# Attention and gated MLP on one core: V evicted into its own partition half, two copies per chunk, and all engines in a new order

## The chip, the core and the metric

One NeuronCore of one Trainium2 chip. The metric is device time in microseconds of one execution, the median over several runs. Engines: TensorE (PE), which multiplies matrices; ScalarE (ACT); VectorE (DVE); GpSimd (POOL); SyncE (SP), which here only issues DMAs. A *chunk* is 512 of the 2048 positions, a *tile* 128 of them.

## What is computed

```python
xn = _layernorm(x, axis=-1)                  # x: [1, 2048, 512], bf16
q = (xn @ wq).reshape(B, S, 32, 16)          # 32 heads of 16
k, v = xn @ wk, xn @ wv                      # one K and V head for all
p = softmax(q @ k^T * 16 ** -0.5)            # per head, 2048 x 2048
s = (p @ v) @ wo
g = silu(silu(xn @ w1) @ w2)                 # MLP, F = 1792
return x + s * g
```

## The kernel before

**Tiling.** Scores are made transposed, keys on partitions and 512 queries in the free dimension, for groups of two heads and 64 keys at a time: one *score group* is four matmuls of 64 rows by 32 columns (lines 1025 to 1036; where the keys stand in the array already, the weight load is left out, line 1030). There are 32 head groups `g` and 64 such score tiles in each, 2048 in all.

**Two ways to the exponential.** A score tile in a bank of PSUM goes to ScalarE, which takes the exponential into `pa_sb` (line 1805, one or two banks in one instruction), or to VectorE, which turns the score into the bits of an approximate power of two in `db_sb` (line 1114). Each batch of eight VectorE tiles is then shifted three times by an integer addition into `ds_sb`, by GpSimd (line 1301) or, near the end, by VectorE (line 1297); the four versions are summed with weights. So V is held in K + 1 = 5 versions, one plain and four scaled by `SHIFT_W`, and beside the 16 columns of V stand 16 constant columns whose product gives the softmax denominator.

**The product with V** (line 1383, in `do_pv`). One step is four matmuls over 64 keys. The rows 0 to 63 of a probability tile and the rows 64 to 127 belong to two parts of the heads, both for the *same* 64 keys. So V of a 64-key block `kb` is wanted on both halves of the partitions, and that is why V is copied. V of a chunk comes out of the projection (line 718) with 128 keys on 128 partitions: even blocks on partitions 0 to 63, odd ones on 64 to 127.

**V's way before.** `mk_V.consume` (lines 724 to 738) evicts a chunk on VectorE with one multiplication into a staging tile, `vg_sb`, all five versions at once (line 726), and SP issues four copies to `v_sb` (line 735): for each half `h` of the staging tile, to both halves `d` of the partitions. A copy's pieces, contiguous on both sides, are 4 tiles x 32 columns x 2 bytes = 256 bytes. The constant columns of `vg_sb` are filled once by GpSimd (line 524). A product step on block `kb` waits for the two copies of its parity (`v_reads`, line 1043). The staging tile is one buffer, so the eviction of a chunk waits for the copies of the chunk before it.

**What sets the order.** Nothing is scheduled at run time. A planner (class `Planner`) plays the kernel through on the host with assumed durations and fixes the order of every engine; each task has its engine, an assumed time, what it reads and writes, and a priority. Names as `T_V` or `T_P` are such assumed times. `SEEDS` is a list of random seeds, one for each 6 us of planned time; a seed of 0 leaves the planner's parameters as they are, another one shakes them, and so picks another order for that stretch. A changed assumed time therefore moves instructions all over the program. The instructions then run in that order on their engine and wait for one another by semaphores; a DMA has one of its own.

**The fill.** LayerNorm of the 16 tiles (lines 577 to 606, VectorE), transposes on TensorE (line 645) and their eviction (656), the K projection (680, evicted by VectorE at 698, and copied once more, shifted by 16 partitions, by a DMA that GpSimd issues at 1440), the V projection (718), and the q projections (copied, shifted by 32 partitions, at 768) come in the first 45 us, mixed with the first scores and products.

Of the kernel before, what the change touches and what calls it, by code (L numbers as in the profile page):

```python
# [10 lines left out]
BF16 = mybir.dt.bfloat16  # L11
# [11 lines left out]
SEEDS, STRETCH = [0, 0, 0, 0, 0, 67544, 0, 0, 0, 363544, 0, 187751, 352584, 0, 0, 643717, 54089, 0, 500791, 0, 175753, 679479, 214263, 0, 883134, 0, 0, 0, 0, 511125, 137466, 261807, 271339, 290944, 259724, 692065, 0, 61765, 0, 164833, 905861, 878832, 719837, 613243, 948977, 4691, 909829, 0, 349743, 92963, 252825, 0, 110717, 997210, 971279, 445136, 398030, 0, 132258, 1132, 474376, 574133, 826754, 871874, 616628, 937227, 803633, 65864, 717197, 436910, 166023, 929504, 484504, 583112, 12539, 430470, 521539, 946998, 894031, 739455, 525815, 630866, 323202, 789653, 301092, 0, 990630, 289782, 266249, 0, 96063, 194209, 222008, 432027, 777900, 662892, 377151, 0, 0, 99687, 0, 586790, 13379, 110492, 494480, 485028, 288231, 0, 0], 6000.0  # L23
# [18 lines left out]
T_V = 250.0  # L42
FIRST = (2, 2, 8, 4)
KU, VG_PRIO, ROOM0 = 0, 0, 4

# [326 lines left out]
def bass_recurrent_scan__grouped_kv_mqa__dense_activation_silu__prompt_kernel(  # L372
# [29 lines left out]
    with ExitStack() as es:  # L402
# [15 lines left out]
        v_sb = sb("v_sb", [P, K + 1, 2, NKB // 2, 2 * DH], BF16)  # L418
# [21 lines left out]
        vg_sb = sb("vg_sb", [P, K + 1, 4, 2 * DH], BF16)  # L440
# [82 lines left out]
        for j in range(K + 1):  # L523
            pl.add(Task(PO, 150.0, lambda g, j=j: g.memset(vg_sb[:, j, :, DH:], 1.0 if j == 0 else SHIFT_W[j - 1]),
                        (), [("Vw", j)], 2, ports=2, gate=lambda: ("st", 0) in pl.lastw and ("st", 3) not in pl.lastw or xn_task[3].op is not None))
# [147 lines left out]
        def mk_K(c, ka, kb, bk=None):  # L673
# [13 lines left out]
            def consume(jb, op):  # L687
                b = jb.bank
                out = []
                for a in range(1):  # L690
# [6 lines left out]
                    else:  # L697
                        t = Task(DV, T_P - (NQ - n) / 0.96, lambda g, dst=dst, a=a: g.tensor_scalar(  # L698
# [13 lines left out]
        def mk_V(c):  # L712
# [11 lines left out]
            def consume(jb, op):  # L724
                b = jb.bank
                t = Task(DV, 410.0, lambda v: v.tensor_tensor(
                    vg_sb[:, :, :, 0:DH],
                    bank(b)[:, 0:4 * DH].rearrange("p (t e) -> p t e", e=DH).unsqueeze(1).to_broadcast([P, K + 1, 4, DH]),
                    wj_sb[:, :].unsqueeze(2).unsqueeze(3).to_broadcast([P, K + 1, 4, DH]), ALU.mult),
                    [("ps", b)] + [("wj", j) for j in range(K + 1)], ["vg"], VG_PRIO)  # L730
                last = t
                for h in range(2):
                    for d in range(2):
                        def emit(e, h=h, d=d):
                            return e.dma_start(v_sb[64 * d:64 * d + 64, :, h, 4 * c:4 * c + 4, :], vg_sb[64 * h:64 * h + 64, :, :, :])  # L735
# [1201 lines left out]
```

## Time and profile before

| | |
|---|---|
| runs shown, us | 663.26, 662.25, 660.95; median 662.25 |
| the profiled execution, us | 662.01; span from first to last instruction 660.2; granted TensorE clock 0.997 |
| busy us: TensorE, VectorE, ScalarE, GpSimd | 648.1, 633.4, 641.3, 573.0 |
| V copies `v_sb<-vg_sb` | 16, 80 KB each |

The profile is one execution. Its views, as they are called below: busy time by stage (each engine's busy time in chosen stretches), the timeline (instructions in order of time, with the idle time ahead of one and what ended it in square brackets), the waits (who waited for whom, in total), the chain of waits (the work that ended last, followed backwards), the DMA issues (size and time from issue to landing) and the groups of instructions by line. Instructions of an engine overlap, since one starts before the one ahead of it has left the pipeline; busy time is counted once.

### The profile page before, as it was taken

What the parts mean: (1) busy time and instruction counts of PE and PEld (TensorE: products, weight loads), DVE (VectorE), ACT (ScalarE), POOL (GpSimd) and SP (SyncE); (2) the same over time, 40 slices, a digit from 0 to 9 for tenths busy, and PEclk for the clock granted to TensorE, in tenths of its full rate; (3) what the DMA queues carried; (4) which work ended last, traced back from release to release, by engine and by line L of the source; (5) the groups of instructions that cost most, each with busy time, mean ns of one, the idle gap of its engine ahead of it and who ended that gap; (6) DMA issues with size and microseconds to landing.
All of it is one profiled execution on the core that took longest, in us unless ns stands there. A gap on an engine that the chain in (4) does not pass through costs nothing.

```text
span 660.2 us, 44477 instructions
## 1 busy us (share of the span) xinstructions
PE 648.1 (98%) x21992; PEld 339.1 (51%) x19600; DVE 633.4 (96%) x1149; ACT 641.3 (97%) x1124; POOL 573.0 (87%) x329
## 2 busy tenths in 40 slices
PE   8889999999999999999999999999999999999997
PEld 3345554555545555664555455455454555455653
DVE  8789999999999999999999999999999999999894
ACT  6789999999999999999999999999999999999996
POOL 3038899999999999999998999998999999988950
PEclk9899999999999999999999999999999999999999
DMA  5531111000011111000000011000000000110001
GB/s 175 160 84 44 36 35 36 10 5 10 5 34 37 27 34 28 5 10 4 11 4 4 11 20 18 13 4 11 4 10 4 10 14 12 29 33 5 4 4 34
DMA packets 17674, 17.23 MB, mean 26 GB/s; under 512 B 7697, under 2 KB 16657, under 8 KB 17297
## 3 DMA queue, kind: packets, MB, share of 16 engines
q1 hardware_dynamic: 15280, 12.10, 6.4%
q0 software_dynamic: 1920, 2.03, 2.4%
q8 instruction: 162, 2.65, 1.7%
q10 hardware_dynamic: 288, 0.26, 0.1%
q14 instruction: 24, 0.19, 0.1%
HBM read 8.95 MB, written 3.67 MB: 19 GB/s over the span
## 4 chain that ended last, share of the span: by engine, by line
PE 94%; DVE 2%; ACT 1%; DMA 1%; issue 0%; SPq 0%
PE ps L1036 31%; PE ps L1383 30%; PE ps L758 20%; PE ps L1030 13%; ACT pa_sb L1805 1%; DVE stats_sb L577 1%; DMA v_sb<-vg_sb 1%; PE ps L1615 1%; PE ps L680 0%; PE ps L645 0%; SPq L735 0%; DVE w_sb L853 0%; PE ps L718 0%; DVE mv_sb L581 0%; DVE xnT_sb L656 0%
## 5 line engine op out<-in xcount | busy, mean ns | idle before, releaser
L1805 ACT ACTIVATE pa_sb<-ps 128x512 bf16<-128x512 f32 (+1 forms) x1034 | 612.4, 768 | 7.6 <-PE ps L1036 6.7
L1301 POOL INT64_ADD ds_sb<-db_sb x297 | 558.5, 1940 | 32.1 <-PE ps L1383 11.7
L1114 DVE TENSOR_SCALAR db_sb<-ps 128x512 uint16<-128x512 f32 x800 | 498.7, 680 | 9.4 <-PE ps L1036 3.4
L1036 PE MATMUL ps<-qt_sb,kt_sb 64*32 64x512 bf16 x5800 | 486.1, 379 | 1.5 <-ACT pa_sb L1805 0.8
L1383 PE MATMUL ps<-ds_sb,v_sb 64*32 64x512 bf16 x4848 | 356.4, 376 | 0.0
L1383 PE MATMUL ps<-pa_sb,v_sb 64*32 64x512 bf16 x2480 | 256.8, 379 | 3.8 <-DMA v_sb<-vg_sb 2.0
L1030 PE MATMUL ps<-qt_sb,kt_sb 64*32 64x512 bf16 x2392 | 231.1, 376 | 0.0
L1036 PEld LDWEIGHTS ps<-qt_sb,kt_sb 64*32 64x32 bf16 x5800 | 139.6, 89 | 160.2 <-ACT pa_sb L1805 71.5
L1383 PE MATMUL ps<-db_sb,v_sb 64*32 64x512 bf16 x1616 | 181.9, 377 | 0.0
L1383 PEld LDWEIGHTS ps<-ds_sb,v_sb 64*32 64x32 bf16 x4848 | 137.9, 91 | 41.3 <-issue 14.8
L758 PE MATMUL ps<-xnT_sb,w_sb 64*32 64x512 bf16 x1792 | 138.8, 377 | 0.0
L758 PE MATMUL ps<-w_sb,u_sb 64*32 64x512 bf16 x1792 | 132.4, 377 | 0.0
L1383 PEld LDWEIGHTS ps<-pa_sb,v_sb 64*32 64x32 bf16 x2480 | 86.3, 91 | 29.4 <-issue 10.3
L1383 PEld LDWEIGHTS ps<-db_sb,v_sb 64*32 64x32 bf16 x1616 | 58.6, 91 | 15.4 <-issue 5.0
L758 PEld LDWEIGHTS ps<-xnT_sb,w_sb 64*32 64x32 bf16 x1792 | 44.1, 91 | 24.7 <-issue 5.2
L758 PEld LDWEIGHTS ps<-w_sb,u_sb 64*32 64x32 bf16 x1792 | 43.3, 91 | 18.3 <-issue 5.1
L814 ACT ACTIVATE t_sb<-ps 128x512 bf16<-128x512 f32 x72 | 49.6, 689 | 0.0
L815 DVE SCALAR_TENSOR_TENSOR u_sb<-t_sb,ps 128x512 bf16<-128x512 bf16 x56 | 37.9, 677 | 0.4 <-ACT t_sb L814 0.4
L758 PE MATMUL ps<-xnT_sb,wq_sb 64*32 64x512 bf16 x480 | 37.3, 377 | 0.0
L758 PE MATMUL ps<-wo_sb,on_sb 64*32 64x512 bf16 x384 | 29.8, 377 | 0.0
L1404 DVE STREAM_TRANSPOSE ps<-ps 128x512 f32<-128x512 f32 (+1 forms) x33 | 23.2, 705 | 5.7 <-PE ps L1383 5.7
L1440 POOL DMA_DIRECT2D kt_sb<-kt_sb x4 | 2.3, 580 | 26.3 <-DVE kt_sb L698 20.3
(75 smaller groups left out, 191.3 us busy)
## 6 DMA issues: line engine op xcount, KB each, us to landing
w_sb<-in_B_w_dram SPq DMA_DIRECT2D x1, 1792.0 KB, 8.8
w_sb<-in_B_w_dram SPq DMA_DIRECT2D x14, 128.0 KB, 2.4
ds_sb<-in_A_x_dram SPq DMA_DIRECT2D x3, 512.0 KB, 6.8
qt_sb<-qt_sb SPq DMA_DIRECT2D x16, 96.0 KB, 2.1
out_dram<-in_A_x_dram SPq DMA_DIRECT2D x12, 128.0 KB, 2.4
out_dram<-ob_sb POOLq DMA_DIRECT2D x12, 128.0 KB, 3.2
v_sb<-vg_sb SPq DMA_DIRECT2D x16, 80.0 KB, 3.0
wq_sb<-in_A_wq_dram SPq DMA_DIRECT2D x1, 512.0 KB, 5.0
```

The lines of the kernel that those rows point to most:

```text
L577: ts_ = pl.add(Task(DV, 593.0, lambda v, t=t: v.bn_stats(stats_sb[:, t, :], x_tile(t)), [xkey(t)], [("st", t)], 1 + j, gate=(lambda j=j: x ...
L758: h = pe.matmul(bank(b)[32 * j:32 * (j + 1), :], lhsT=lhs(k, rows, 32 * j, 32), rhs=rhs(k, rows), start=first, stop=last, tile_position=(r ...
L814: t1 = Task(AC, T_AF + 0.8333 * NQ, lambda a: a.activation(t_sb[:, k, :], bank(b), ACT.Tanh, scale=scale), [("ps", b)], [("t", k)], 0)
L815: t2 = Task(DV, T_P, lambda v: v.scalar_tensor_tensor(out=dst, in0=t_sb[:, k, :], scalar=1.0, in1=bank(b), op0=ALU.add, op1=ALU.mult), [(" ...
L1030: h = pe.add_instruction(mybir.InstMatmult(name=pe.bass.get_next_instruction_name(), engine=mybir.EngineType.PE, ins=[pe.lower_ap(q), pe.l ...
L1036: h = pe.matmul(to, lhsT=keys, rhs=q, start=True, stop=True, tile_position=(r0, 32 * j), skip_group_check=True)
L1114: bt.P[k] = pl.add(Task(DV, T_P, lambda v: v.tensor_scalar(db_sb[:, bt.b, k * NQ:(k + 1) * NQ], bank(b), 128.0 * LOG2E, 128.0 * (SHIFT_BET ...
L1301: whole["po"].append(pl.add(Task(PO, T_P64, lambda g: g.int64_add(ds_sb[:, s, :].bitcast(U64), db_sb[:, bt.b, :].bitcast(U64), words), rea ...
L1383: h = pe.matmul(bank(OB)[q:q + 32, :], lhsT=lhs[rows], rhs=rhs[rows], start=s0, stop=s1, tile_position=(64 * l, q), skip_group_check=True)
L1404: t1 = pl.add(Task(DV, (T_TR - 60.0) / parts + 60.0, lambda v, cols=cols: v.transpose(bank(OB)[:, cols], bank(OB)[:, cols]), [("ps", OB)], ...
L1615: h = pe.matmul(bank(tb[r])[32 * j:32 * (j + 1), :], lhsT=on_cols(oi % NON, slice(r0, r0 + 64), r * P + 32 * j, 32), rhs=wo_sb[r0:r0 + 64, ...
L1805: op = pl.place(AC, 0.8333 * NQ * n + T_AF, lambda a: a.activation(pa3[:, k0:k1 + 1:max(1, k1 - k0), :], ps3[:, b0:b1 + 1:step, :], ACT.Ex ...
```

## The change

V is evicted straight into `v_sb`, which now has a leading index of two: index 0 holds, on each half of the partitions, the blocks that the projection put there; index 1 holds the blocks of the other half. Only index 1 is copied, by two DMAs per chunk that swap the halves within `v_sb`. The order of the dimensions is changed so that a chunk's 5 versions x 4 tiles x 32 columns are contiguous: pieces of 1280 bytes. `vg_sb` is gone. GpSimd fills the constant columns of all four chunks in index 0 (256 elements per version where it was 64). A product step now reads index 0 on one half and index 1 on the other, and waits for both copies of the chunk. In the planner, the assumed times of the V projection and of K's eviction change, SP's DMA issues are taken at 600 ns (they were 60 or 100), and `SEEDS` is another list; so every engine has another order.

```diff
-T_V = 250.0
+T_V, T_VE, V_KB = 220.0, 410.0, 150
+T_SP = 600.0
...
-        v_sb = sb("v_sb", [P, K + 1, 2, NKB // 2, 2 * DH], BF16)
+        v_sb = sb("v_sb", [P, 2, NC, K + 1, 4, 2 * DH], BF16)
...
-        vg_sb = sb("vg_sb", [P, K + 1, 4, 2 * DH], BF16)
...
-            pl.add(Task(PO, 150.0, lambda g, j=j: g.memset(vg_sb[:, j, :, DH:], 1.0 if j == 0 else SHIFT_W[j - 1]),
+            pl.add(Task(PO, T_MS / 2, lambda g, j=j: g.memset(v_sb[:, 0, :, j, :, DH:], 1.0 if j == 0 else SHIFT_W[j - 1]),
...
-                        t = Task(DV, T_P - (NQ - n) / 0.96, lambda g, dst=dst, a=a: g.tensor_scalar(
+                        t = Task(DV, T_P + 60.0 - (NQ - n) / 0.96, lambda g, dst=dst, a=a: g.tensor_scalar(
...
-                t = Task(DV, 410.0, lambda v: v.tensor_tensor(
-                    vg_sb[:, :, :, 0:DH],
+                t = last = Task(DV, T_VE, lambda v: v.tensor_tensor(
+                    v_sb[:, 0, c, :, :, 0:DH],
...
-                    [("ps", b)] + [("wj", j) for j in range(K + 1)], ["vg"], VG_PRIO)
-                last = t
-                for h in range(2):
-                    for d in range(2):
-                        def emit(e, h=h, d=d):
-                            return e.dma_start(v_sb[64 * d:64 * d + 64, :, h, 4 * c:4 * c + 4, :], vg_sb[64 * h:64 * h + 64, :, :, :])
-                        last = pl.add(Task(SP, 100.0, emit, ["vg"] + [("Vw", j) for j in range(K + 1)], [("V", 2 * h + d, c)], -1, [last], dma=80 * 1024))
+                    [("ps", b)] + [("wj", j) for j in range(K + 1)] + [("Vw", j) for j in range(K + 1)], [("V", 0, c)], VG_PRIO)
+                for d in range(2):
+                    last = pl.add(Task(SP, T_SP, lambda e, d=d: e.dma_start(
+                        v_sb[64 * d:64 * d + 64, 1, c, :, :, :], v_sb[64 - 64 * d:P - 64 * d, 0, c, :, :, :]),
+                        [("V", 0, c)], [("V", 1 + d, c)], -1, [last], dma=V_KB * 1024))
...
-            return v_sb[:, j, kb % 2, kb // 2, :]
+            return lambda rows: v_sb[rows, (kb % 2) ^ (rows.start // 64), kb // 8, j, kb // 2 % 4, :]
...
-            return [("V", 2 * (kb % 2) + d, kb // 8) for d in range(2)]
+            return [("V", d, kb // 8) for d in range(3)]
...
-                        h = pe.matmul(bank(OB)[q:q + 32, :], lhsT=lhs[rows], rhs=rhs[rows], start=s0, stop=s1,
+                        h = pe.matmul(bank(OB)[q:q + 32, :], lhsT=lhs(rows), rhs=rhs[rows], start=s0, stop=s1,
```

The q copies (line 768), the stores and the loads of x get `T_SP` as their assumed time in place of 60.0.

**Three places of the order.** First TensorE at its first product with V, before and after. `d27` to `d30` before, and `d27` and `d28` after, are the semaphores of chunk 0's copies; `q_ACT` and `q_DVE` stand for results of ScalarE and VectorE; line 645 (646 after) is a transpose, 1383 (1382) the product, 1036 (1035) and 1030 (1029) scores.

```order
L1036 MATMUL ps<-qt_sb,kt_sb 32x512 [waits q_ACT]
L1036 MATMUL ps<-qt_sb,kt_sb 32x512 x3
L645 MATMUL ps<-ident,xn_sb 128x128 [waits q_DVE]
L645 MATMUL ps<-ident,xn_sb 128x128 x7
L645 MATMUL ps<-ident,xn_sb 128x128 [waits q_ACT,q_DVE]
L645 MATMUL ps<-ident,xn_sb 128x128 x7
L1383 MATMUL ps<-pa_sb,v_sb 32x512 [waits d28,d27,d29,d30]
L1383 MATMUL ps<-pa_sb,v_sb 32x512 x3
L1036 MATMUL ps<-qt_sb,kt_sb 32x512 x4
```

The same place after:

```order
L646 MATMUL ps<-ident,xn_sb 128x128 [waits q_DVE]
L646 MATMUL ps<-ident,xn_sb 128x128 x7
L1035 MATMUL ps<-qt_sb,kt_sb 32x512 [waits q_ACT]
L1035 MATMUL ps<-qt_sb,kt_sb 32x512 x3
L646 MATMUL ps<-ident,xn_sb 128x128 [waits q_DVE]
L646 MATMUL ps<-ident,xn_sb 128x128 x7
L1382 MATMUL ps<-pa_sb,v_sb 32x512 [waits d27,d28]
L1382 MATMUL ps<-pa_sb,v_sb 32x512 x3
L1035 MATMUL ps<-qt_sb,kt_sb 32x512 [waits q_ACT]
L1035 MATMUL ps<-qt_sb,kt_sb 32x512 x3
```

The product stood behind a score and two transposes and waited for four copies; now a score stands between the transposes, and the product waits for two copies. Second, TensorE at its first product with chunk 2, before (`d36` and `d37` are the first two of that chunk's four copies):

```order
L1383 MATMUL ps<-pa_sb,v_sb 32x512 x2
L1030 MATMUL ps<-qt_sb,kt_sb 32x512 [waits q_DVE]
L1030 MATMUL ps<-qt_sb,kt_sb 32x512 x3
L1383 MATMUL ps<-pa_sb,v_sb 32x512 [waits d36,d37,q_ACT]
L1383 MATMUL ps<-pa_sb,v_sb 32x512 x3
L1036 MATMUL ps<-qt_sb,kt_sb 32x512 x4
```

And after (`d32` and `d33` are both of its copies):

```order
L1382 MATMUL ps<-pa_sb,v_sb 32x512 x2
L1035 MATMUL ps<-qt_sb,kt_sb 32x512 [waits q_ACT]
L1035 MATMUL ps<-qt_sb,kt_sb 32x512 x3
L1382 MATMUL ps<-db_sb,v_sb 32x512 [waits d32,d33,q_DVE]
L1382 MATMUL ps<-pa_sb,v_sb 32x512
L1382 MATMUL ps<-db_sb,v_sb 32x512
L1382 MATMUL ps<-pa_sb,v_sb 32x512
```

The first product that reads chunk 2 used ScalarE's tiles and now uses a tile of VectorE beside one of ScalarE, at about the same point of the row: 42 rows behind the V projection of that chunk before, 43 after. Third, VectorE around the eviction of chunk 2, before:

```order
L602 TENSOR_TENSOR var_sb<-var_sb 128x4 [waits q_DVE]
L698 TENSOR_SCALAR kt_sb<-ps,part_sb 128x512 [waits q_PE]
L603 SCALAR_TENSOR_TENSOR rstd_sb<-var_sb,rstd_sb 128x4 [waits q_DVE]
L606 TENSOR_SCALAR xn_sb<-ds_sb,mv_sb,rstd_sb 128x512 [waits q_DVE]
L726 TENSOR_TENSOR vg_sb<-ps,wj_sb 128x20x16 [waits d33,d34,d32,d35,q_PE]
L606 TENSOR_SCALAR xn_sb<-ds_sb,mv_sb,rstd_sb 128x512 x3
L1114 TENSOR_SCALAR db_sb<-ps 128x512 [waits q_PE]
```

And after:

```order
L699 TENSOR_SCALAR kt_sb<-ps,part_sb 128x512 [waits q_PE]
L603 TENSOR_TENSOR var_sb<-var_sb 128x4 [waits q_DVE]
L727 TENSOR_TENSOR v_sb<-ps,wj_sb 128x20x16 [waits q_PE]
L604 SCALAR_TENSOR_TENSOR rstd_sb<-var_sb,rstd_sb 128x4 [waits q_DVE]
L1113 TENSOR_SCALAR db_sb<-ps 128x512 [waits q_PE]
L607 TENSOR_SCALAR xn_sb<-ds_sb,mv_sb,rstd_sb 128x512 [waits q_DVE]
L607 TENSOR_SCALAR xn_sb<-ds_sb,mv_sb,rstd_sb 128x512 x3
```

The eviction of V (line 726, 727 after) has moved ahead of one step of the reciprocal root and of the first normalising pass (606, 607), and no longer waits for four copies of the chunk before. SP's order is the same at this place but for four V copies per chunk that become two, ahead of the load of w1 in the first chunk; on GpSimd the five fills stand where they stood, three ahead of a wait for VectorE and two behind it, where it was four and one.

More of the change, by code (lines that the diff above doesn't have):

```diff
@@ L885, in add_xr @@
             if tt < NT - 4:
[L886 removed]
+                xr_task[tt] = pl.add(Task(SP, T_SP, lambda e: e.dma_start(ov[:, tt, :], xv[:, tt, :]),
                                           (), [("out", tt)], 2, [], dma=256 * 1024))
```

9 lines of the change are left out of this document (4 added, 5 removed).

## The prediction

> **What bounds the kernel now.** I read first a table of busy time by stage, cut where the engines change their behaviour: the fill, then the 600 us in which everything runs at once, then the tail. Columns: busy us of TensorE, weight loads, VectorE, ScalarE, GpSimd, each with its count of instructions, then TensorE's granted clock, the share of the DMA engines and GB/s.
>
> ```profile
> core 0: us, PE busy (x) PEld busy (x) DVE busy (x) ACT busy (x) POOL busy (x), PEclk, DMA share, GB/s
> 0.00:11.50 11.50, 9.49 (x140) 4.68 (x140) 9.92 (x57) 5.96 (x13) 3.64 (x16) 1.00 0.78 233
> 11.50:20.60 9.10, 6.66 (x106) 2.62 (x92) 8.72 (x31) 9.04 (x13) 1.77 (x2) 1.00 0.32 70
> 20.60:25.60 5.00, 3.97 (x72) 1.30 (x64) 1.96 (x6) 1.62 (x2) 0.00 (x0) 0.66 0.90 345
> 25.60:36.20 10.60, 10.49 (x230) 4.80 (x178) 10.00 (x29) 9.98 (x16) 1.08 (x2) 1.00 0.32 80
> 36.20:41.00 4.80, 3.56 (x88) 1.58 (x74) 2.85 (x5) 2.46 (x5) 0.37 (x1) 1.00 0.10 23
> 41.00:50.00 9.00, 8.50 (x256) 3.79 (x230) 8.35 (x14) 8.48 (x17) 5.78 (x4) 1.00 0.41 109
> 50.00:651.40 601.40, 601.40 (x21094) 319.07 (x18778) 587.24 (x1000) 601.17 (x1056) 560.35 (x306) 1.00 0.07 16
> 651.40:660.20 8.80, 3.99 (x60) 1.28 (x48) 4.35 (x14) 2.57 (x6) 0.00 (x0) 0.95 0.18 61
> ```
>
> ScalarE is the measure: from 50 to 651.4 us it rests 0.23 us in 601.40, and the tail of 8.80 us begins where its last exponential ends. The work behind that is fixed:
>
> ```profile
> L1805 ACT ACTIVATE pa_sb<-ps 128x512 bf16<-128x512 f32 (+1 forms) x1034 | 612.4, 768 | 7.6 <-PE ps L1036 6.7
> ```
>
> The order of the changed kernel holds the same 1034 exponentials, 828 single and 206 double as before, and the same 72 tanh. So the end moves by what ScalarE loses or wins elsewhere, and between its first exponential and 50 us it is idle 0.06 + 3.38 + 0.62 + 2.34 + 0.52 = 6.92 us. That is about the most the fill can give. Two places hold 5.72 us of it, 20.6 to 25.6 and 36.2 to 41; VectorE and TensorE are idle there too.
>
> Next, the timeline of TensorE at these two places (start, length, line, tiles, count, idle before):
>
> ```profile
> 16.92 0.40 PE L1036 MATMUL ps<-qt_sb,kt_sb 64*32 64x512 bf16 x4 [0.52 <-ACT pa_sb L1805]
> 18.33 1.27 PE L645 MATMUL ps<-ident,xn_sb 128*128 128x128 bf16 x16
> 21.63 0.62 PE L1383 MATMUL ps<-pa_sb,v_sb 64*32 64x512 bf16 x4 [2.03 <-DMA v_sb<-vg_sb]
> 22.02 0.64 PE L1383 MATMUL ps<-pa_sb,v_sb 64*32 64x512 bf16 x4
> 23.88 1.32 PE L680 MATMUL ps<-xnT_sb,wke_sb 128*32 128x512 bf16 x16
> 25.13 0.40 PE L1383 MATMUL ps<-pa_sb,v_sb 64*32 64x512 bf16 x4
> 25.36 0.39 PE L1383 MATMUL ps<-pa_sb,v_sb 64*32 64x512 bf16 x4
> 30.38 1.05 PE L680 MATMUL ps<-xnT_sb,wke_sb 128*32 128x512 bf16 x16
> 37.49 0.40 PE L1383 MATMUL ps<-pa_sb,v_sb 64*32 64x512 bf16 x4 [1.24 <-issue]
> ```
>
> At 19.60 (18.33 + 1.27) TensorE has done the transposes and stands 2.03 us before the first product with V, for the copies of V's chunk 0. At 36.25 it stands 1.24 us more. The view puts that down to "issue", but I read the same cause: this product is the first to read chunk 2 and waits for its first two copies, and the queue's rows, looked at one at a time, give the landing of the second:
>
> ```profile
> 16.49 0.63 SPq L735 DMA_DIRECT2D v_sb<-vg_sb  x1
> 17.83 3.75 DMA v_sb<-vg_sb
> 33.81 0.62 SPq L735 DMA_DIRECT2D v_sb<-vg_sb  x1
> v_sb<-vg_sb SPq DMA_DIRECT2D x1, 80.0 KB, 3.6
> ```
>
> The last line is that of the copy issued at 33.81: 33.81 + 3.6 = 37.41, and TensorE goes on at 37.49. For chunk 0 the second of the four copies is issued at 16.49; the fourth, at 17.83, takes 3.75 us and lands at 21.58.
>
> **The change part by part.** *Two copies for four, 1280 bytes for 256.* The eviction of V (four, x4) keeps its shape and, for chunk 0, its place in VectorE's order; it is one pass of the same elements, so I cost it at nothing. The two halves that were copied in place are gone; the two left go out in the first two issue slots. What a copy of this kind takes is bounded by the q copies (KB each, median us from issue to landing) and by the V copies of now:
>
> ```profile
> qt_sb<-qt_sb SPq DMA_DIRECT2D x16, 96.0 KB, 2.1
> DMA to landing us min/median/max: 2.2/3.0/4.1
> ```
>
> The q copies go from partition to partition within the core in pieces of 1024 bytes, as the new V copies will in pieces of 1280; so I take 2.1, with 4.1 as the bad end. Second copy of chunk 0: issued at 16.49, landed at 18.6 (bad end 20.6). TensorE comes for it at 19.60, so the wait of 2.03 us goes (bad end: 1.0 us stays). What is next late there: the transposes, which read what VectorE writes until 18.91 (17.53 + 1.38, a row below), and they set 19.60 already.
>
> *The clock.* After the stall TensorE ran at a granted 0.66 in 20.6 to 25.6: product steps 21.63 to 22.02 are 0.39 apart against 25.13 to 25.36, 0.23, and the K projection takes 1.32 against 1.05. From 21.63 to 25.13 TensorE did five product groups and that projection in 3.50 us; 23.88 − 21.63 = 2.25 halves to about 1.15, and the projection's step of 1.25 to about 1.0, so 1.35 us less if the clock stays up. From 11.5 to 20.6 TensorE was busy 6.66 of 9.10 us at a clock of 1.00, so gaps of the kind that remain did not lower it. Bounds: 0 and 1.35; I take 1.2, since ScalarE is not fed sooner by all of it. [...]
>
> *Chunk 2.* In the new order VectorE evicts it ahead of a LayerNorm pass that stood before it, so the second copy is issued at 33.81 at the latest and lands at 35.9 (+ 2.1), before TensorE's 36.25: 1.24 us go; bad end (3.6 again) nothing goes. Chunks 1 and 3 had no wait of note and keep none; that the eviction no longer shares one buffer takes away waits that cost nothing (VectorE shows none there).
>
> ScalarE's and VectorE's side of the same places:
>
> ```profile
> 17.53 1.38 DVE L606 TENSOR_SCALAR xn_sb<-ds_sb,mv_sb,rstd_sb 128x512 bf16<-128x512 bf16 x4
> 11.56 9.04 ACT L1805 ACTIVATE pa_sb<-ps 128x512 bf16<-128x512 f32 x13 [0.50 <-PE ps L1036]
> 22.32 0.60 ACT L1805 ACTIVATE pa_sb<-ps 128x512 bf16<-128x512 f32 x1 [1.73 <-PE ps L1036]
> 23.59 1.02 ACT L1805 ACTIVATE pa_sb<-ps 128x1024 bf16<-128x1024 f32 x1 [0.67 <-PE ps L1030]
> 25.61 6.82 ACT L1805 ACTIVATE pa_sb<-ps 128x512 bf16<-128x512 f32 x10 [1.00 <-PE ps L1036]
> 37.97 1.23 ACT L1805 ACTIVATE pa_sb<-ps 128x512 bf16<-128x512 f32 x2 [1.26 <-PE ps L1036]
> 25.26 0.75 DVE L698 TENSOR_SCALAR kt_sb<-ps,part_sb 128x512 bf16<-128x512 f32 x1 [3.04 <-PE ps L680]
> 38.16 0.69 DVE L1114 TENSOR_SCALAR db_sb<-ps 128x512 uint16<-128x512 f32 x1 [1.05 <-PE ps L1030]
> ```
>
> ScalarE's three pauses add to 3.40 us at the first place: 2.0 + 1.2 = 3.2 of them go. At the second its 1.26 us go. VectorE's two pauses, 3.04 and 1.05, cover 4.1 us of a gain of 4.4; beyond that VectorE's own passes of this stage come late, and I give back 0.4 us for it.
>
> *GpSimd's fills.* Five fills of V's constant columns grow from 64 to 256 elements, and in the new order two, not one, stand behind the LayerNorm passes:
>
> ```profile
> 8.80 0.15 POOL L524 MEMSET vg_sb<- 128x64 bf16 x1 [5.14 <-DVE xn_sb L606]
> 8.89 1.92 POOL L539 MEMSET qt_sb<- 128x512 bf16 x4
> 12.87 0.72 POOL L1440 DMA_DIRECT2D kt_sb<-kt_sb  x1 [0.32 <-POOL kt_sb L536]
> ```
>
> By 0.15 for 64 and 0.48 for 512 elements a fill takes some 0.3 us, so the copy of K's chunk 0 is issued at about 13.4 rather than 12.87. Its reader on TensorE stood at 16.9; 13.4 + 2.1 = 15.5 is cover of over 1 us. Cost 0; without the cover, up to 0.5.
>
> *The w1 load* (1792 KB, next in SP's queue) goes out two issue slots of 0.63 us sooner. If its traffic meets V's second copy, that is the 4.1 us end above: 1.0 us.
>
> *The new order of everything else.* The work is the same but for one shift pass that goes from VectorE to GpSimd, which has 41 us of room in the long stretch (560.35 of 601.40), and 136 weight loads fewer, which lie beside matmuls. The 0.23 us that ScalarE rests can't shrink. But pauses shorter than the overlap of two instructions don't show:
>
> ```profile
> 103.01 0.69 ACT L814 ACTIVATE t_sb<-ps 128x512 bf16<-128x512 f32 x1
> 103.49 1.13 ACT L1805 ACTIVATE pa_sb<-ps 128x1024 bf16<-128x1024 f32 x1
> ```
>
> A single lasts 0.69 and the next starts 0.48 after it, so up to 0.2 us each could hide; 2 ns more or less on each of the 1056 make 2 us. I take 0, with ±2.
>
> Sum, on the profiled execution's own 662.0 us (span 660.2 and 1.8 around it; the median of the runs, 662.25, is 0.2 above): − 2.0 − 1.2 − 1.2 + 0.4 = − 4.0, so **658.0 us**.
>
> **The rivals.** *A: part of it stays.* Either the pieces' size buys nothing, or the clock drops all the same. In the first case chunk 2's copy takes 3.6 again and 1.2 stays: 659.2. For it: the shortest V copy of now, in 256-byte pieces, took 2.2 us too, so the long ones may only have queued. Against: 2.1 at 1024-byte pieces. [...] In the second case 1.2 is lost as well: 659.2. For it: TensorE stays thinly fed around 19 us. Both together: 660.4.
>
> *B: the gain is spent in the stage or by the new order.* VectorE's 4.1 us of pauses are the limit of the fill; if its passes then gate TensorE, or ScalarE picks up short pauses later, 2 to 4 us go back: 660.0 to 662.0.
>
> *C: slower, by starving ScalarE in the long stretch.* The profile's waits:
>
> ```profile
> ACT pa_sb L1805 <- PE ps L1036: 6.7, 9, 1.7
> PEld ps L1036 <- ACT pa_sb L1805: 71.5, 298, 0.9
> ```
>
> A score that comes late costs ScalarE 6.7 / 9 = 0.74 us. The new order has other places at which a group of heads ends and the next output bank is taken; if nine scores are late there, 6.7 us come on top of − 4.0: 664.7. It decides from nine on (+ 2.7); five or fewer leave a gain. Against it: TensorE waits for ScalarE to free a bank 298 times, so the scores run ahead.
>
> **How the numbers follow.** The forecast gets 0.54, A 0.24, B 0.13, C 0.09. The range must leave out C and a part of B: high 661.2. Low: the forecast with 2 us won by the new order, 656.0. Runs of this kernel tell 0.3%, 2.0 us, from no change: faster means below 660.2, which is the forecast and nearly all of A less a little for its ends: 0.74; same 0.17 (B and the rest of A); slower 0.09.
>
> **What would show it.** Right: no wait of TensorE on a V copy by 20 us; V copies landing in about 2.1 us; a granted clock of 1.00 from 20 to 26 us; ScalarE's idle time before 50 us near 2.5 us; the stretch after it without pauses and as long as now. Wrong: V copies at 3 us or more, a clock below 0.8 after 20 us, VectorE without a pause from 20 to 41 us while TensorE waits for it, or ScalarE idle by more than 2 us after 50 us.

## The result, and the profile after

The changed kernel takes **656.86 us** (median of 4 runs, 655.99 to 657.70) against 662.18 for the kernel before (median of 4, 660.95 to 663.26): a ratio of 0.992, 95% interval 0.9896 to 0.9944, which is 5.3 us less. The forecast was 658.0 in a range of 656.0 to 661.2. The execution profiled after took 657.56 us with a span of 655.7, against 662.01 and 660.2. One run of the kernel before, among those of the second group below, took 965.8 us at a granted clock of 0.655; the ratios, and the 42 runs counted further down, leave it out.

Busy time by stage after the change, cut as in the prediction; the columns are the same (TensorE, weight loads, VectorE, ScalarE, GpSimd, granted clock, DMA share, GB/s):

```profile
11.50:20.60 9.10, 7.45 (x128) 3.05 (x120) 8.72 (x30) 8.48 (x12) 2.11 (x2) 1.00 0.26 54
20.60:25.60 5.00, 5.00 (x111) 2.35 (x91) 5.00 (x14) 4.55 (x7) 0.55 (x1) 1.00 0.97 375
25.60:36.20 10.60, 10.51 (x251) 4.63 (x212) 9.96 (x26) 9.25 (x17) 0.80 (x2) 1.00 0.17 43
36.20:41.00 4.80, 4.80 (x142) 2.01 (x118) 4.63 (x8) 4.80 (x10) 2.29 (x3) 1.00 0.23 61
41.00:50.00 9.00, 9.00 (x316) 4.97 (x279) 9.00 (x17) 9.00 (x18) 8.65 (x5) 1.00 0.29 84
50.00:646.80 596.80, 596.56 (x20904) 327.42 (x18472) 579.86 (x988) 595.92 (x1048) 557.91 (x305) 1.00 0.07 16
646.80:655.70 8.90, 4.42 (x76) 1.50 (x60) 4.36 (x14) 3.00 (x6) 0.00 (x0) 0.99 0.18 62
```

From 20.6 to 25.6 us, where ScalarE had worked 1.62 us of 5.00 at a granted clock of 0.66, it now works 4.55 at 1.00; from 36.2 to 41 it worked 2.46 of 4.80 and now 4.80. (The same work comes sooner now, the K projection of 38.48 us at 33.78, so the stages agree in their times and not in their work; the sum over them counts.) Between 11.5 and 50 us it is idle 0.62 + 0.45 + 1.35 = 2.42 us where it was 6.92. The long stretch and the tail are nearly as they were: 0.88 us idle in 596.80 (0.23 in 601.40 before), and 8.90 us after 646.8 where it had been 8.80. So the time came out of the fill.

TensorE at its first product with V, and V's copies (start, length, what, idle before; then KB each and median us to landing of all eight, and the time that an issue takes on SP, min/median/max ns):

```profile
18.74 0.62 PE L646 MATMUL ps<-ident,xn_sb 128*128 128x128 bf16 x8 [0.58 <-DVE xn_sb L607]
19.62 0.62 PE L646 MATMUL ps<-ident,xn_sb 128*128 128x128 bf16 x8
20.17 0.40 PE L1382 MATMUL ps<-pa_sb,v_sb 64*32 64x512 bf16 x4
20.40 0.39 PE L1382 MATMUL ps<-pa_sb,v_sb 64*32 64x512 bf16 x4
21.36 1.05 PE L681 MATMUL ps<-xnT_sb,wke_sb 128*32 128x512 bf16 x16
```

```profile
v_sb<-v_sb SPq DMA_DIRECT2D x8, 80.0 KB, 2.2
```

```profile
L733 SPq DMA_DIRECT2D v_sb<-v_sb x8: 461/551/607, 16.2 to 36.7; - x8
```

The product at 20.17 follows the transposes with no idle time; the step to the next product is 0.23 and the K projection takes 1.05, as at a granted clock of 1.00 before. The median of 2.2 us hides two copies, those of chunk 1:

```profile
v_sb<-v_sb SPq DMA_DIRECT2D x2, 80.0 KB, 3.7
```

They took 3.8 and 3.5 us, by the prediction a sign of being wrong ("V copies at 3 us or more"), and cost nothing, since they had landed by 28.4 us and the first product with that chunk came at 29.08. ScalarE's pauses in the fill are what is left:

```profile
12.00 8.48 ACT L1804 ACTIVATE pa_sb<-ps 128x512 bf16<-128x512 f32 x11 [0.50 <-PE ps L1035]
20.65 2.00 ACT L1804 ACTIVATE pa_sb<-ps 128x1024 bf16<-128x1024 f32 x3 [0.17 <-PE ps L1035]
22.82 0.60 ACT L1804 ACTIVATE pa_sb<-ps 128x512 bf16<-128x512 f32 x1 [0.17 <-PE ps L1035]
29.34 5.01 ACT L1804 ACTIVATE pa_sb<-ps 128x512 bf16<-128x512 f32 x9 [0.23 <-PE ps L1035]
35.24 0.60 ACT L1804 ACTIVATE pa_sb<-ps 128x512 bf16<-128x512 f32 x1 [0.89 <-PE ps L1035]
36.07 4.45 ACT L1804 ACTIVATE pa_sb<-ps 128x512 bf16<-128x512 f32 x8 [0.23 <-PE ps L1035]
```

Before, the largest pauses were 1.73, 1.00 and 1.26 us; now one of 0.89 stands out; it stands behind the K projection of 33.78, as one of 0.74 us did at 39.94 before. The first exponential starts at 12.00 where it started at 11.56. That is scatter between executions: the same order started it at 11.68 in another execution of this kernel.

### The profile page after: what moved, and what is told of

It is laid out like the page before. It is cut to its first block, busy times and chain, and to the rows that moved or that the text cites. A ratio compares the mean times of both kernels' runs of the same rounds, so it can differ in the third digit from the quotient of the medians.

```text
span 655.7 us, 44308 instructions
## 1 busy us (share of the span) xinstructions
PE 647.9 (99%) x21992; PEld 351.0 (54%) x19464; DVE 631.0 (96%) x1147; ACT 641.0 (98%) x1124; POOL 576.5 (88%) x330
## 3 DMA queue, kind: packets, MB, share of 16 engines
q0 software_dynamic: 1920, 2.03, 2.4%
## 4 chain that ended last, share of the span: by engine, by line
PE 86%; ACT 12%; DVE 2%; issue 0%
PE ps L1382 29%; PE ps L1035 25%; PE ps L757 18%; ACT pa_sb L1804 11%; PE ps L1029 11%; PE ps L1757 1%; DVE stats_sb L578 1%; PE ps L1614 1%; PE ps L646 0%; PE ps L681 0%; ACT t_sb L813 0%; PE ps L719 0%; DVE w_sb L852 0%; DVE xnT_sb L657 0%; DVE xn_sb L607 0%
## 5 line engine op out<-in xcount | busy, mean ns | idle before, releaser
L1382 PE MATMUL ps<-pa_sb,v_sb 64*32 64x512 bf16 x2480 | 264.4, 377 | 0.1
L1382 PE MATMUL ps<-db_sb,v_sb 64*32 64x512 bf16 x1616 | 192.9, 376 | 0.0
L1382 PEld LDWEIGHTS ps<-ds_sb,v_sb 64*32 64x32 bf16 x4848 | 142.8, 91 | 44.4 <-issue 10.4
L757 PE MATMUL ps<-w_sb,u_sb 64*32 64x512 bf16 x1792 | 135.7, 377 | 0.0
L757 PE MATMUL ps<-xnT_sb,w_sb 64*32 64x512 bf16 x1792 | 135.2, 377 | 0.0
L1382 PEld LDWEIGHTS ps<-pa_sb,v_sb 64*32 64x32 bf16 x2480 | 91.1, 91 | 31.7 <-issue 10.8
L1382 PEld LDWEIGHTS ps<-db_sb,v_sb 64*32 64x32 bf16 x1616 | 64.5, 91 | 14.0 <-issue 2.4
```

Source lines behind the costliest of these rows:

```text
L757: h = pe.matmul(bank(b)[32 * j:32 * (j + 1), :], lhsT=lhs(k, rows, 32 * j, 32), rhs=rhs(k, rows), start=first, stop=last, tile_position=(r ...
L1382: h = pe.matmul(bank(OB)[q:q + 32, :], lhsT=lhs(rows), rhs=rhs[rows], start=s0, stop=s1, tile_position=(64 * l, q), skip_group_check=True)
```

## The experiments

Three things change at once: the path of V (two copies for four), the size of the pieces (1280 bytes for 256), and the order of all engines. My theory was the prediction's: the path removes two waits, and the order is worth nothing. The rivals: the order makes the gain; the size of the pieces buys nothing, or everything. In the expectations T1, T2 and T3 stand for the prediction's terms: the wait at chunk 0 (− 2.0), the clock (− 1.2) and chunk 2 (− 1.2). Kernels of one group ran on one chip, beside the kernel before, and each ratio is to that: its median was 662.89 us in the first group (e1 to e4), 662.65 in the second (e5 to e7 and the changed kernel again), 662.26 in the third (e8, e9). The last column is ScalarE's idle time from 11.5 to 50 us in the one execution that was profiled; it was 6.92 us in the kernel before and 2.42 in the changed one.

| kernel | copies a chunk | piece, bytes | order | median us | ratio (95%) | ScalarE idle, us |
|---|---|---|---|---|---|---|
| changed kernel, second group | 2 | 1280 | new | 656.52 | 0.9917 (0.9897 to 0.9938) | 2.52 |
| e1 | 2 | 1280 | old | 658.10 | 0.9919 (0.9894 to 0.9944) | 1.89 |
| e2 | 4 | 256 | new | 662.24 | 0.9991 (0.9973 to 1.0010) | 6.66 |
| e3 | 2 | 256 | new | 658.14 | 0.9922 (0.9897 to 0.9947) | 3.36 |
| e4 | none | - | new | 657.41 | 0.9903 (0.9877 to 0.9929) | 2.09 |
| e5 | 4 | 1280 | new | 660.42 | 0.9970 (0.9957 to 0.9983) | 5.39 |
| e6, chunk 0 late | 2 | 1280 | old | 661.53 | 0.9993 (0.9975 to 1.0010) | 6.17 |
| e7, chunk 2 late | 2 | 1280 | old | 659.05 | 0.9945 (0.9928 to 0.9962) | 3.68 |
| e8, loads sooner | 2 | 1280 | new | 656.62 | 0.9911 (0.9887 to 0.9935) | 2.21 |
| e9, loads sooner | 4 | 1280 | new | 659.32 | 0.9950 (0.9933 to 0.9968) | 5.17 |

### The path in the old order, and the old path in the new order

e1 takes the kernel before and, once its order is planned, drops the two copies within a half and lets the eviction write index 0. A product step waits there, as before, for the copies of its own parity alone, now one, where the changed kernel waits for both:

```diff
-                    vg_sb[:, :, :, 0:DH],
+                    v_sb[:, 0, c, :, :, 0:DH],
...
+    for e, v in pl.order.items():
+        v[:] = [o for o in v if id(o) not in gone]
```

> V is evicted into its own partition half and copied in two copies of 1280-byte pieces, as in the changed kernel, but every engine keeps the order of the kernel before. If the path is what pays (the prediction's terms T1 to T3): the two copies of chunk 0 are issued at about 16.0 and 16.6 us and have landed by 19.0, before the product at 19.6; the copies of chunk 2 are issued at about 33.2 and 33.8 and have landed by 36.0, before 36.25; so the waits of 2.03 and 1.24 us and the cold clock at 20.6 to 25.6 go, ScalarE's idle time between 11.5 and 50 us falls from 6.9 to about 2.5, and the time is 657 to 658.5 us. If the new order is what pays: the stalls go only in part and the time stays at 660.5 to 662. If the order also costs something at the head (the first exponential came 0.44 us later in the changed kernel), this kernel starts its first exponential at 11.56 again and is as fast as the changed one or up to 0.4 us faster, 656.4 to 656.9.

Measured: 0.9919, the ratio of the changed kernel. TensorE and ScalarE in e1:

```profile
18.33 1.27 PE L644 MATMUL ps<-ident,xn_sb 128*128 128x128 bf16 x16
19.53 0.40 PE L1384 MATMUL ps<-pa_sb,v_sb 64*32 64x512 bf16 x4
```

```profile
11.56 10.45 ACT L1806 ACTIVATE pa_sb<-ps 128x512 bf16<-128x512 f32 x15 [0.50 <-PE ps L1037]
22.17 6.82 ACT L1806 ACTIVATE pa_sb<-ps 128x512 bf16<-128x512 f32 x10 [0.17 <-PE ps L1037]
```

The first product comes straight after the transposes, in the very place where the kernel before stood still for 2.03 us, and ScalarE's pauses of 1.73, 0.67 and 1.00 us there shrink to one of 0.17. The order isn't needed for this. Chunk 2 is another matter. Its two copies in e1, issued at 29.74 and 30.24:

```profile
v_sb<-v_sb SPq DMA_DIRECT2D x1, 80.0 KB, 2.0
...
v_sb<-v_sb SPq DMA_DIRECT2D x1, 80.0 KB, 3.6
```

The first product with chunk 2 starts at 32.42 without a wait, but it needs only the first copy, which landed at 31.79; the second landed at 33.86. Had it waited for both, as the changed kernel does, it would have stood some 1.4 us. So e1 shows that the old order loses nothing with a wait for one copy; the old order with the changed kernel's wait was not run.

e2 is the reverse: the order of the changed kernel, with the staging tile and four copies put back.

```diff
-                    v_sb[:, 0, c, :, :, 0:DH],
+                    vg_sb[:, :, :, 0:DH],
...
+                p.emit, p.deps = o.emit.copy(h, 1, c), list(o.deps)
+                new.append(p)
```

> The staging tile and the four copies per chunk in pieces of 256 bytes, as before, in the order of the changed kernel. If the path is what pays: four issues of 0.63 us from 16.2 us and 3.75 us to land put the last copy of chunk 0 at about 21.7 us, 1.5 us after the product wants it at 20.17; a wait of about 1.5 us there with a lower granted clock behind it (1.2 us in the kernel before); chunk 2, evicted at 29.0, lands at about 34.4, 1.4 us after 33.03; in all 3 to 4 us more than the changed kernel, 660 to 661 us. If the order is what pays: it leaves room for the slower copies, no wait of over 0.5 us, and 656.9 to 657.5 us.

Measured: 0.9991; the whole gain is gone, some 1 us more than I gave, and ScalarE is idle 6.66 us in the fill. The timeline of TensorE in e2, and its stage from 20.6 us:

```profile
22.01 0.40 PE L1395 MATMUL ps<-pa_sb,v_sb 64*32 64x512 bf16 x4 [1.73 <-DMA v_sb<-vg_sb]
36.90 0.39 PE L1395 MATMUL ps<-pa_sb,v_sb 64*32 64x512 bf16 x2 [0.51 <-DMA v_sb<-vg_sb]
44.64 0.37 PE L1395 MATMUL ps<-db_sb,v_sb 64*32 64x512 bf16 x1 [0.70 <-DMA v_sb<-vg_sb]
```

```profile
20.60:25.60 5.00, 3.59 (x92) 1.73 (x88) 3.31 (x8) 2.71 (x5) 0.23 (x1) 1.00 0.79 273
```

Three waits on V copies, the first of 1.73 us, near the 1.5 expected; but the granted clock stays at 1.00 behind it in this execution, so the cold clock of the prediction does not follow from such a wait each time. More time is lost later, in chunk 3 too, for which I had named no wait.

### Is it the pieces or the number of copies?

e3 keeps two copies and the order, but lays V out so that a copy moves pieces of 256 bytes; e5 keeps pieces of 1280 and issues two more copies ahead of the two of each chunk; e4 has no copies.

```diff
-        v_sb = sb("v_sb", [P, 2, NC, K + 1, 4, 2 * DH], BF16)
+        v_sb = sb("v_sb", [P, 2, K + 1, NC, 4, 2 * DH], BF16)
```

> The changed kernel, its order and its two copies per chunk, with V laid out so that each copy moves pieces of 256 bytes, five to a partition, where the changed kernel has one of 1280. If the size of the pieces sets how long a copy takes: 3.0 us to land (the median of the kernel before) and up to 3.75 for chunk 0, so that its second copy lands at about 20.5 us, a wait of about 0.3 us before the product at 20.17, and 657 to 657.6 us. If the number of copies in flight sets it: 2.2 us to land as in the changed kernel, no wait, and 656.9 us. Both times lie close, so the landing times decide.

Measured: 0.9922, not told from the changed kernel's 0.9917. Its copies of chunk 0, and the second copy of chunk 2:

```profile
v_sb<-v_sb SPq DMA_DIRECT2D x2, 80.0 KB, 2.3
```

```profile
v_sb<-v_sb SPq DMA_DIRECT2D x1, 80.0 KB, 4.0
```

At chunk 0 they land in 2.3 us (2.0 and 2.1 in pieces of 1280) and nothing waits, as the second theory had it. The second copy of chunk 2 took 4.0 and landed at 33.7, some 0.5 us after the eviction by VectorE (33.16) to which the view puts the wait down; chunk 3 cost 0.43. That execution, at 660.02 us, was the slowest of the six. On the median, small pieces cost 0.3 us (0.0005 of 662), which is not told from nothing; the intervals leave some 2 us of doubt.

e5 inserts, ahead of each chunk's first copy:

```diff
+                return e.dma_start(dum_sb[64 * d:64 * d + 64, s, :, :, :], v_sb[64 - 64 * d:P - 64 * d, 0, c, :, :, :])
```

> The changed kernel with two more copies of the same size issued ahead of the two of each chunk, into a tile that nothing reads: four copies per chunk as before, but in pieces of 1280 bytes. If the number of issues is what delays the last copy: it is issued at about 17.9 instead of 16.7 us and lands, at 2.2 us a copy, at about 20.1, just when the product wants it (20.17 in the changed kernel): a wait of 0 to 0.4 us at each of chunks 0, 2 and 3, ScalarE's idle time before 50 us 2.4 to 3.6, and 657 to 658.3 us; the four copies in small pieces cost 4 us more than that only since both add up. If four copies in flight also slow one another: 3 us to land, waits of about 1 us, 659 to 661 us.

Measured: 0.9970, 3.5 us more than the changed kernel, though every piece is 1280 bytes: the second theory's time. TensorE's waits in e5:

```profile
21.08 0.40 PE L1392 MATMUL ps<-pa_sb,v_sb 64*32 64x512 bf16 x4 [1.24 <-DMA v_sb<-v_sb]
35.43 0.37 PE L1392 MATMUL ps<-db_sb,v_sb 64*32 64x512 bf16 x1 [1.32 <-DMA v_sb<-v_sb]
43.62 0.39 PE L1392 MATMUL ps<-db_sb,v_sb 64*32 64x512 bf16 x1 [0.72 <-DMA v_sb<-v_sb]
```

They add to 3.3 us. Of the copies, the first three of chunk 0 land in 2.0, 2.1 and 2.1 us; the fourth, issued at 17.59, takes 3.4:

```profile
v_sb<-v_sb SPq DMA_DIRECT2D x1, 80.0 KB, 3.4
```

So the number of copies decides most of it (3.5 us), and the size of the pieces hardly matters (0.3 us in e3); between e5 and e2, which has pieces of 256 bytes and the staging tile too, lie 0.0021 (1.4 us), and their intervals overlap. But why does the fourth take longer than the third? That is the last section of the experiments.

e4 takes all eight copies out; both halves of the product read what the eviction wrote, so it leaves the exchange of V between the halves out:

```diff
-                    last = pl.add(Task(SP, T_SP, lambda e, d=d: e.dma_start(
-                        v_sb[64 * d:64 * d + 64, 1, c, :, :, :], v_sb[64 - 64 * d:P - 64 * d, 0, c, :, :, :]),
+                    last = pl.add(Task(SP, T_SP, copied,
...
-            return lambda rows: v_sb[rows, (kb % 2) ^ (rows.start // 64), kb // 8, j, kb // 2 % 4, :]
+            return lambda rows: v_sb[rows, 0, kb // 8, j, kb // 2 % 4, :]
```

> The changed kernel without the eight V copies: both partition halves of the product read the half that the eviction writes, so this kernel leaves the exchange of V between the partition halves out. If what is left of the copies is hidden, as the prediction has it: the same time as the changed kernel, 656.6 to 657.1 us, and ScalarE's idle time between 11.5 and 50 us stays at about 2.4 us. If the copies still cost something (queue places ahead of the w1 load, their DMA traffic): w1 still goes out at 18.7 us since it waits for LayerNorm, and the time falls by up to 0.5 us.

Measured: 0.9903 against 0.9917 and 0.992: at most some 1 us less, within the intervals. ScalarE is idle 2.09 us from 11.5 to 50 us with no copies at all, 2.42 and 2.52 with two. Little more is to be had from V's copies.

### Each wait by itself

e6 and e7 are e1 with small extra copies (16 KB, to a tile that nobody reads) issued ahead of the two copies of chunk 0, or of chunk 2:

```diff
+LATE = {0: 5}
...
+            for n in range(LATE.get(t[2], 0)):
+                new.append(p)
```

> The new path in the old order, with five extra copies of 256 bytes per partition, into a tile that nothing reads, issued ahead of the two V copies of chunk 0 alone: these are issued some 2.9 us later and land at about 21.5 us, where the product wants them at 19.5: the wait of the kernel before, by itself. By the prediction's terms T1 and T2 (the wait, and the cold clock that follows it) the time is 2.0 + 1.2 = 3.2 us above the same kernel without them, with a granted clock of about 0.66 in 20.6 to 25.6. If the clock does not follow from such a wait alone (the kernel with the old path in the new order waited 1.73 us there at a granted clock of 1.00): 2.0 us above, clock 1.00.

Measured: 0.9993, that is 4.9 us above e1 (ratios 0.9919 and 0.9993, each within about 0.002). TensorE and a stretch behind the wait in e6:

```profile
22.71 0.40 PE L1392 MATMUL ps<-pa_sb,v_sb 64*32 64x512 bf16 x4 [2.77 <-DMA v_sb<-v_sb]
```

```profile
22.00:23.00 1.00, 0.29 (x16) 0.22 (x20) 0.56 (x1) 0.00 (x0) 0.00 (x0) 1.00 0.80 118
24.00:25.00 1.00, 1.00 (x12) 0.35 (x16) 0.00 (x0) 0.85 (x1) 0.00 (x0) 0.50 0.97 391
26.00:27.00 1.00, 1.00 (x24) 0.17 (x8) 1.00 (x3) 0.57 (x1) 0.08 (x1) 0.50 1.04 426
```

The wait came out longer than meant, 2.77 us, and the clock went to 0.50 more than a microsecond after TensorE had started again: the first theory, wait and clock together, and 1.7 us more than it gave, 0.74 of them the longer wait. One late chunk brings the whole time of the kernel before back.

> The new path in the old order, with three extra copies of 256 bytes per partition ahead of the two V copies of chunk 2 alone: these are issued some 1.7 us later, at 31.5 and 32.0 us, and the second lands at about 34.1, where the product wants it at 32.6: a wait of about 1.5 us there and nowhere else. By the prediction's term T3 (the 1.24 us that the profile called issue were a wait on these copies, and ScalarE lost them in full) the time is about 1.3 to 1.6 us above the same kernel without them. If ScalarE's queue of scores covers it: no more than 0.5 us above.

The same with `LATE = {2: 3}`. Measured: 0.9945, 1.7 us above e1, as the first theory had it, though the two intervals overlap. TensorE and ScalarE in e7:

```profile
34.56 0.40 PE L1392 MATMUL ps<-pa_sb,v_sb 64*32 64x512 bf16 x4 [1.64 <-DMA v_sb<-v_sb]
```

```profile
35.03 1.23 ACT L1814 ACTIVATE pa_sb<-ps 128x512 bf16<-128x512 f32 x2 [1.66 <-PE ps L1045]
```

A wait of 1.64 us of TensorE is a pause of 1.66 us of ScalarE: no queue of scores covers it, and ScalarE's idle time in the fill is 1.8 us above e1's. The two profiled executions differ by 0.3 us alone (spans 655.3 and 655.0), since e1's has more pauses after 50 us; so the price in the whole time rests on the medians. The same product, ps<-pa_sb,v_sb, stood 1.24 us under the label "issue" in the kernel before.

> The changed kernel once more, on the chip and beside the runs with which the others of this call are compared: a ratio to the kernel before of 0.992, the new path in the old order being no faster and no slower than it by more than 0.3%.

Measured: 0.9917, against 0.9919 of e1: no difference. In the execution profiled here the second copy of chunk 2 took 3.4 us and landed at 33.14, and its product waited, again under "issue":

```profile
v_sb<-v_sb SPq DMA_DIRECT2D x1, 80.0 KB, 3.4
```

```profile
33.23 0.37 PE L1382 MATMUL ps<-db_sb,v_sb 64*32 64x512 bf16 x1 [0.31 <-issue]
```

So the wait at chunk 2 is not always gone.

### What makes a copy take 3 us and more

Copies that took 2.0 to 2.4 us and such that took 3 and more stood in all kernels that copy V. The slow ones were in flight together with a packet of 16 KB of the queue "instruction", called a load of instructions here: one started in the quarter microsecond from 18.75 us before and after the change (18.98 and 18.77). Its row in the changed kernel for that quarter (packets, MB, the packets' time as a share of 16 engines):

```profile
q8 instruction: 1, 0.02, 23.6%
```

23.6% of 16 x 0.25 us is 0.94 us for this one packet. The two copies of the changed kernel have landed by 18.8 (issued at 16.17 and 16.72, 2.0 and 2.1 us); of the kernel before, the third and the fourth had not, and took 4.1 and 3.8. In e6 the five small copies of 16 KB, one after another, with a load at 18.35 and the DMA queue of the copies taking 11 to 18% of the DMA engines' time (17.3 to 18.9 us), show it best. Those issued at 16.1, 17.3 and 17.9, and then the second real copy, issued at 20.55:

```profile
dum_sb<-v_sb SPq DMA_DIRECT2D x1, 16.0 KB, 1.7
...
dum_sb<-v_sb SPq DMA_DIRECT2D x1, 16.0 KB, 3.2
...
dum_sb<-v_sb SPq DMA_DIRECT2D x1, 16.0 KB, 2.8
...
v_sb<-v_sb SPq DMA_DIRECT2D x1, 80.0 KB, 2.1
```

A copy of a fifth of the bytes takes 3.2 us ahead of the load, and one behind it 2.1, though it is the seventh in the row.

It is the moment that counts, not the mere overlap. The traces of all kernels hold 128 copies out of V's tiles, the extra ones included. Of these, 69 had such a load start between 0.4 us before and 1.45 us after their issue, and every one of them took 2.5 to 4.1 us. Of the other 59, many of which a load met near the end of their flight, 56 took 1.7 to 2.4, and three, with a load 1.6 to 2.1 us after the issue, 4.0 to 4.2. The copy that held the product of chunk 2 is a case of it. It is the second of its row before the change and after it; it took 3.6 us before (load 1.2 us after the issue), 2.3 in the changed kernel (1.7 after) and 3.4 in the same kernel's other profile (1.3 after).

To test this I moved the loads, by adding instructions at the head of TensorE's stream.

```diff
+                    if 3 <= n <= 9:
+                        return None
+                    for k in range(26 if n == 2 else 1):
+                        h = pe.matmul(bank(6)[:, 0:32 if n == 2 else NQ], lhsT=zer_sb[:, 0:P],
```

> The changed kernel with eight of TensorE's 20 warm-up products at the start (their result is read by nobody) replaced by 26 of 32 columns: 18 products and 18 weight loads more ahead of the work, so that each 16 KB load of instructions comes about 1.3 us sooner, near 17.4 instead of 18.75 us and near 30.2 instead of 31.5. If a load in flight holds up the copies that are in flight with it (the copies that took 3 us and more in these runs crossed one): the two V copies of chunk 0, issued at 16 to 17, take 2.8 to 3.5 us instead of 2.0, and so do those of chunk 2, issued at 29.2 and 29.8; the second copies land at about 20.0 and 33.0, where the products want them at about 20 and 32.9, a wait of 0 to 0.6 us each, and the time is 657 to 658.2 us. If it was the place in the row of copies or the w1 load behind them: the copies keep their 2.0 to 2.2 us, and the time stays at 656.5 to 657.

Measured: the load comes 2.3 us sooner (18.77 to 16.45; the copies come 0.6 sooner in this execution), and the first and the second copy of chunk 0 in e8, the same copies in the same places, now take

```profile
v_sb<-v_sb SPq DMA_DIRECT2D x1, 80.0 KB, 3.1
...
v_sb<-v_sb SPq DMA_DIRECT2D x1, 80.0 KB, 2.8
```

instead of 2.0 and 2.1; the w1 load is issued behind them as before, at 18.14. So with the load moved into their flight, these two took 1.1 and 0.7 us longer: a load does hold up the copies. My time for it was wrong: the second copy, issued at 16.14, lands at 18.9 and is still in time; of the waits that I expected only one of 0.19 us at 32.82 came. 0.9911 is the ratio of the changed kernel.

> The kernel with four copies of 1280-byte pieces per chunk, with the same 36 TensorE instructions more at the start. There the copy that the product waits for, the fourth, is issued at about 17.5 us (chunk 0) and 32.1 us (chunk 2), a little ahead of the instruction loads at 18.5 and 32.5. If a load in flight holds copies up: with the loads 1.3 us sooner, at about 17.2 and 31.2, these two copies reach the queues when the load is nearly done and land in 2.2 to 2.8 us instead of 3.5; the waits of 1.24 and 1.32 us shrink by 0.7 to 1.2 us each, and the time falls by 1.2 to 2.4 us against the same kernel without the instructions, 658 to 659.2 us: the shift that costs the kernel with two copies time helps the one with four. If the place in the row of copies or the w1 load slows them: nothing changes, 660.4 us.

Measured: 0.9950 against 0.9970 of e5: the intervals overlap, and TensorE's waits in e9, in an execution that was the slowest of eleven (661.49 us), are nearly those of e5:

```profile
20.86 0.40 PE L1392 MATMUL ps<-pa_sb,v_sb 64*32 64x512 bf16 x4 [1.08 <-DMA v_sb<-v_sb]
35.23 0.37 PE L1392 MATMUL ps<-db_sb,v_sb 64*32 64x512 bf16 x1 [1.34 <-DMA v_sb<-v_sb]
```

The fourth copy of chunk 0 did land in 2.1 us, as expected. But it was issued only at 18.69, since SP's issue of the second extra copy, begun at 16.25 just ahead of the load (16.48), held the queue:

```profile
L718 SPq DMA_DIRECT2D dum_sb<-v_sb x8: 461/550/1754, 15.7 to 38.9; - x8
```

1754 ns where the median is 550. And at chunk 2 the load came only 0.7 us sooner (31.90) and still met the fourth copy. This kernel did not turn the sign as I had expected; the long issue, if the load is its cause, is a second way in which a load delays copies.

## Why the prediction was right, point by point

- **ScalarE is the measure, and the fill is where the change acts**: right. Its idle time before 50 us fell by 4.5 us, the profiled spans by 4.5 (660.2 to 655.7); the long stretch stayed full.
- **The wait of 2.03 us at chunk 0 goes**: right; there is no idle time ahead of the product at 20.17. e1 and e2 show that the path does it, in either order: with two copies there is no wait at chunk 0, with four one of 1.73 or 2.03 us.
- **"So I take 2.1"**: the number was right (2.0 and 2.1 at chunk 0, 2.2 the median), its ground only in part. I took 2.1 from pieces of 1024 bytes; e3 has 2.3 with 256. The copies of chunk 0 land soon since they are the first two in the row and are through before the load of instructions at 18.77; those of chunk 1 meet a load and take 3.8 and 3.5. The first half of rival A was right on the pieces and wrong on what follows: by it 1.2 us would have stayed at chunk 2, where 0 and 0.31 did.
- **The cold clock, − 1.2**: right for the profiled pair (0.66 before, 1.00 after), but not a fixed cost of the wait. e2 waits 1.73 us at a clock of 1.00, and of the 42 runs of the kernel before in the first two groups 12 had a mean clock of 0.999 or 1.000, at 662.0 us on average, and 19 one of 0.997 or less, at 663.7. That is a difference of 1.7 us between executions. The longer the wait at chunk 0, the more often the clock was low (a stretch of 3.4 us at 0.50, as in the profiles of the kernel before, 21.1 to 24.5 us, and of e6, 23.9 to 27.3, takes 0.0026 off the mean): a mean clock of 0.997 or less came in 9 of 12 runs of e6 (wait at chunk 0 of 2.77 us in its profile), 19 of 42 of the kernel before (2.03), 5 of 12 of e2 (1.73), 2 of 12 of e5 (1.24), none of 11 of e9 (1.08), and none of the 34 of the changed kernel, e1, e3, e4 and e8, which have no wait there (e7, with its wait at chunk 2: 1 of 9). By these averages the term is worth 1.7 us in some 45 of 100 executions of the kernel before, 0.8 on the whole; that the forecast started from an execution that had it is luck. What makes the clock fall behind a wait in one execution and not in the next is not shown.
- **Chunk 2, − 1.2, and "issue" read as a wait on a copy**: right. e7 makes the wait with copies alone and prices it at ScalarE one for one. But the fall from 3.6 to 2.1 us, which the prediction took from the larger pieces, was luck: the copy stands second in its row before and after, and took 2.3 or 3.4 us as a load fell. What holds is the ground that V is evicted sooner: TensorE was ready for the product 3.1 us after the eviction's end before the change (33.15 to 36.25), and 3.75 in the changed kernel's other profile (29.17 to 32.92), so that even 3.4 us to land left a wait of 0.31 only. e1 has no wait in the old order, but its product waits for one copy alone.
- **The give-back of 0.4 for VectorE's pauses**: did not come. VectorE works 5.00 of 5.00 us from 20.6 to 25.6 and TensorE 5.00 as well; ScalarE's pauses there are of 0.17 to 0.23 us.
- **GpSimd's fills, 0**: right. They take 0.31 us each (forecast 0.3), and K's copy is issued at 13.21 (13.4); nobody waits for it.
- **The w1 load "goes out two issue slots of 0.63 us sooner"**: wrong, without effect. It goes out at 18.71 us, not before 18.50, because it waits for a LayerNorm result and not for its place in the queue.
- **The new order, 0 ± 2**: e1 against the changed kernel, 0.9919 and 0.9917, puts it at nothing, within some 2 us, as far as e1's wait for one copy at chunk 2 does not hide a part of what the order gives there. Rivals B and C found no ground: no VectorE-bound stage, 0.88 us of pauses after 50 us.
- **The sum**: − 4.0 forecast, − 4.45 in the profiled pair, − 5.3 to − 6.1 on the medians (662.18 to 656.86, and 662.65 to 656.52). The term that looks too small is chunk 0's. e6 prices a wait of 2.77 us there at 4.9 us; less the 0.74 that it is longer than 2.03, that is 4.2 where I had 2.0 + 1.2. With e7 scaled to 1.24 us, 1.3, it makes 5.5. The intervals of e1 and e6 leave some 2 us of doubt on it, and e6 met the low clock in 9 of 12 runs, the kernel before in 19 of 42; so the excess is a likely reading, and not shown.

## What to carry to other kernels

When a bound engine is idle in a fill, price the copies that its feeder waits for by the landing of the *last* one: here its place in the queue times the time of an issue (0.55 us) plus its landing (2.2 us, both medians in the changed kernel). Two copies more were worth 3.5 us (e5), and fivefold pieces no more than the runs can tell (0.3 us, e3). If such a landing takes 1 us longer than its neighbours with the same bytes (3.4 against 2.1 us in e5), look at what else crossed the DMA engines in that microsecond, instruction loads among it, before blaming size or count. And price a wait at the profiled clock and at 1.00: the runs of the kernel before with a mean clock of 0.997 or less took 1.7 us more than those at 0.999 or 1.000.

## What the runs showed of the hardware

- The packet of a load of 16 KB of instructions took 0.88 to 1.53 us in the fill of the changed kernel (22.0% of 16 x 0.25 us from 31.50, 38.3% from 25.25) and 1.42 in e8 (35.6% from 24.00). The copies out of V's tiles that were issued in the 1.45 us ahead of a load's start, or up to 0.4 behind it, landed in 2.5 to 4.1 us (69 of 69), most others in 1.7 to 2.4 (56 of 59). With 36 instructions more at the head of TensorE's stream, the load at 18.77 us came at 16.45 (e8).
- An issue of such a copy on SP that began between 0.25 us ahead of a load's start and 0.4 behind it took 1.2 to 1.75 us in all 14 cases, instead of 0.5 to 0.7: 1754 ns in e9 (begun at 16.25), 1307 in e6, 1340 in the kernel before; 607 at most for V's copies in the changed kernel. That the load is the cause of the long issue was not tried by itself, and the w1 load's issue, begun 0.06 us ahead of a load (18.71), took 0.37 there.
- The granted clock behind a wait was 0.50 for 3.4 us in the profiled executions of e6 (a wait of 2.77 us) and of the kernel before (2.03), and 1.00 in that of e2 (1.73). It differed between executions: a mean of 0.997 or less in 9 of 12 runs of e6, 19 of 42 of the kernel before and 5 of 12 of e2.
